# Attention and feed-forward in one kernel: a written order of 712 pieces up to the second chunk, own buffers for the first four pairs, maxima subtracted by TensorE

## The chip, the cores and the metric

The kernel runs on one core of a Trainium2 chip. The metric is the device time of one execution in microseconds (us). Three executions of the kernel before gave 937.13, 939.01 and 940.65 us; their median, 939.01 us, is the time before. The engines are called by their names in the profile: PE (TensorE, with its weight loads PEld), DVE (VectorE), ACT (ScalarE), POOL (GpSimd) and SP (SyncE, which issues the transfers).

## The reference

For 8 batches, 8 heads, 576 positions and head dimension 64, two attentions are added: one over pooled positions (means of 4, so 144 of them, repeated 4 times in the output) and one over a band of |i-j| < 4. Their sum, 4608 rows of 512, goes through a feed-forward layer with 2048 hidden units and a piecewise quadratic gate.

```python
out_d = sm_attn(q_d, k_d, v_d)              # pooled by 4
out_up = np.repeat(out_d, factor, axis=2)
scores = scale * np.matmul(q, k.transpose(0, 1, 3, 2))
scores = np.where(np.abs(pos[:, None] - pos[None, :]) < factor, scores, -1000000000.0)
...                                         # softmax, then @ v
x = (out_up + out_local).transpose(0, 2, 1, 3).reshape(4608, 512)
h = x @ w_in
g = np.where(h >= 1, h, np.where(h <= -1, 0.0, (h + 1) ** 2 / 4.0))
return g @ w_out
```

## The kernel before

**Attention.** Heads go in pairs: 32 pairs, four for each batch. For a pair, the band scores are formed in ten windows of 64 (`sl_ps`, L224), the pooled scores in three blocks of 48 rows (`sp_ps`, L259). DVE takes the maxima (L243 or L249, L275, L276) and subtracts the band maxima (L244; for pairs 4 to 7 POOL does, L250), ACT takes the exponentials (L251, L279), DVE normalises (L288 to L294), PE turns the weights (`tl_ps` L313, `tp_ps` L325), ACT copies them (L317, L331), PE multiplies them with the values (`pl_ps`, L357 and L369), and DVE adds the two attentions to `x` (L380). ACT rounds `x` to `xh` (L396) and POOL forms the rest `xl = x - xh` (L397), so that a float32 product can be made of three products of rounded parts. The sums of four queries and keys are `qd` (L199) and `kd` (L203); those of the values are `vd` (POOL, L306 and L307; DVE, L301, for pairs 4 to 7).

**Feed-forward.** Weights come as 32 blocks of 512 KB (`raw_i`, `raw_o`, loaded by L592) and are converted: ACT scales both words (L604, L606), DVE shifts and adds (L609, L610), ACT rounds (L612), POOL forms the rest (L613). The tokens go in chunks: chunk 0 has 512, then come eight of 384 and two of 512. For a chunk and one of 16 blocks of hidden units, `mm1` makes 12 products into `h_ps` (L679), the gate runs on DVE, ACT, DVE, ACT and POOL (for chunk 0 L694, L695, L696, L705, L706; later chunks have a copy L699 ahead), and `mm2` makes 12 (or 9) products into `o_ps` (L722). Later chunks overlap with the attention of pairs 8 to 31, which `join` runs one step behind another at the steps listed in `JOINS`.

**What sets the order.** Before chunk 1 the program is traced in the order of two lists of short steps (`BEFORE_STEPS` for pairs 0 to 3, `FIRST_STEPS` for pairs 4 to 7 beside chunk 0; `a0` is the next stage of pair 0, `w` a load of two weight blocks, `c` a conversion, `s` one `mm1` with its gate, `m` one `mm2`), and a scheduler then sorts the instructions of each engine by its own estimates. Every engine takes its instructions strictly in the order of its own queue; an instruction that waits holds all behind it on that engine, and on SP a load that waits for a buffer holds all later loads. Pairs 1 and 3 borrow buffers of late weight blocks (`second`), pairs 0 and 2 share another set; all four share one buffer for `v` and one for the pooled `v`. PSUM has four double banks for pairs 0 to 3; afterwards two banks hold `h_ps`, four `o_ps`, and one double bank the attention.

Of the kernel before, what the change touches and what calls it, by code (L numbers as in the profile page):

```python
# [62 lines left out]
def place(h, g):  # L63
# [39 lines left out]
JOINS = [17, 20, 23, 26, 30, 37, 44, 51, 58, 65, 69, 73, 78, 84, 91, 98, 105, 113, 117, 121, 125]  # L103
JOINS += [129, 133, 137, 142]
# [14 lines left out]
def attention_then_ffn(ctx: ExitStack, tc, qT, kT, vw, vp, vq, band, w_in, w_out, out):  # L119
# [25 lines left out]
    def load(n, name):  # L145
# [16 lines left out]
        loaded[name] = t
# [25 lines left out]
    def attention(n, pool):  # L188

        b, p = pairs[n]  # L190
        q, k = qk[p] if b == 0 else (loaded["q"], loaded["k"])
        copy = nc.scalar.copy


        qd = first_qd
        if n < NPAIR and n % 2:
            qd = scratch(n, [P, NQB * QB + D - QB], "qd", "qd")
            nc.gpsimd.memset(qd[:, SD:], 0.0)
# [4 lines left out]
        nc.vector.tensor_reduce(kd, k.rearrange("p (s f) -> p s f", f=FACTOR), axis=AX.X, op=ALU.add)  # L203
# [16 lines left out]
        for h, r, g in SCORE_ORDER:  # L220
            w = WIN_START[r * NG + g]
            hs = slice(h * D, (h + 1) * D)
            x, c = place(h, g), (2 * g + r) * WIN
            nc.tensor.matmul(  # L224
                sl_v[x * WIN : (x + 1) * WIN, c : c + WIN],
                q[hs, w : w + WIN],
                k[hs, w : w + WIN],
                start=not early,
                stop=True,
                skip_group_check=early,  # L230
            )
        if n + 1 >= NPAIR:
            load(n + 1, "q")
            load(n + 1, "k")
        yield

        sl = scratch(n, [P, NG, 2, WIN], "sl", "sl")
        slf = sl.rearrange("p g r c -> p (g r) c")
        sl_n = sl_v.rearrange("p (n c) -> p n c", c=WIN)
        ml = small(NB, "mxl")  # L240
        ml_n = ml.unsqueeze(2).broadcast_to([P, NB, WIN])
        if early:
            nc.vector.tensor_reduce(ml, sl_n, axis=AX.X, op=ALU.max)  # L243
            nc.vector.tensor_tensor(slf, sl_n, ml_n, op=ALU.subtract)  # L244
        else:
            nc.vector.tensor_tensor(
                slf, sl_n, band_sb.unsqueeze(1).broadcast_to([P, NB, WIN]), op=ALU.add
            )
            nc.vector.tensor_reduce(ml, slf, axis=AX.X, op=ALU.max)  # L249
            nc.gpsimd.tensor_tensor(slf, slf, ml_n, op=ALU.subtract)  # L250
        nc.scalar.activation(slf, slf, AF.Exp, scale=0.125)  # L251
        yield
        sp_ps = pool.tile([P, 2, 512], F32, name="sp_ps", tag="a")
        sp_v = sp_ps[:, 0, 0 : 2 * SD].rearrange("p (n s) -> p n s", n=2)
        sp_w = sp_ps[:, 1, 0:SD]
        for i in (0, 2, 1):
            for h in range(2):
                hs = slice(h * D, (h + 1) * D)
                nc.tensor.matmul(  # L259
                    sp_v[hs, i, :] if i < 2 else sp_w[(1 - h) * D : (2 - h) * D, :],  # L260
                    qd[hs, i * QB : i * QB + D],
                    kd[hs, :],
                    start=True,
                    stop=True,
                )
# [9 lines left out]
        nc.vector.tensor_reduce(mx_ps[:, 2:3], sp_w, axis=AX.X, op=ALU.max)  # L275
        nc.vector.tensor_reduce(mx_ps[:, 0:2], sp_v, axis=AX.X, op=ALU.max)  # L276
# [12 lines left out]
        nc.vector.tensor_scalar_add(sums, sums, 1e-9)
        nc.vector.reciprocal(sums, sums)  # L290
        nc.vector.tensor_tensor(
            slf, slf, sums[:, 0:NB].unsqueeze(2).broadcast_to([P, NB, WIN]), op=ALU.mult
        )
        nc.vector.tensor_tensor(  # L294
# [540 lines left out]
```

## Time and profile before

| what | value |
|---|---|
| median of three runs | 939.01 us |
| the profiled execution, device time | 938.05 us |
| its span, first to last instruction | 936.3 us |
| mean granted PE clock over the span | 0.976 |
| PE, DVE, ACT, POOL busy | 894.3, 494.6, 460.2, 380.1 us |
| bytes moved by the DMA engines | 68.59 MB |

The device time is 1.75 us above the span. In the rows of the profile an arrow points from inputs to the output (`o_ps<-w_o,gh`), the times of one instruction are nanoseconds, and the figures behind a bar are busy time and mean. Window rows give, for each stretch, the busy time of every engine with its instructions in brackets, then the granted PE clock, the share of the DMA engines and GB/s.

### The profile page before, as it was taken

To read this page: it belongs to the slowest core of one execution; us is meant where nothing else is said; L and a number is where in the kernel's file an instruction comes from. 1 tells how busy PE (TensorE), PEld (TensorE's weight loads), DVE (VectorE), ACT (ScalarE), POOL (GpSimd) and SP (SyncE) were. 2 spreads that over 40 slices of the span, in tenths; PEclk is the share of its full clock that TensorE was granted. 3 is DMA by queue.
4 is the path that set the end of the run, shared out by engine and by line. 5 is a ranking of instruction groups with operands and counts; after the bars stand their busy time and mean duration, and the time that the engine had idled before them with its cause. 6 is when DMAs were issued, how large, how long until landed. Compare 5 with 4: busy or idle time off the path is not lost.

```text
span 936.3 us, 18293 instructions
## 1 busy us (share of the span) xinstructions
PE 894.3 (96%) x7420; PEld 795.4 (85%) x7420; DVE 494.6 (53%) x884; ACT 460.2 (49%) x987; POOL 380.1 (41%) x346
## 2 busy tenths in 40 slices
PE   4689899999999999999999999999999999999997
PEld 4567677888999999989999999998998988888886
DVE  5978788567543554366544553456676521212221
ACT  4889554445544444445444444454454443334333
POOL 2647576445433444344433443344544422222221
PEclk7669999999999999999999999999999999999999
DMA  8786111232120121032120121022231000001001
GB/s 293 258 311 210 51 31 39 92 93 79 57 91 1 57 91 57 3 129 75 57 75 18 57 91 40 18 91 75 81 106 57 15 35 1 1 1 46 1 1 45
DMA packets 27973, 68.59 MB, mean 73 GB/s; under 512 B 3248, under 2 KB 3248, under 8 KB 27888
## 3 DMA queue, kind: packets, MB, share of 16 engines
q1 hardware_dynamic: 27888, 67.42, 21.8%
q8 instruction: 58, 0.95, 0.4%
q14 instruction: 27, 0.22, 0.1%
HBM read 57.97 MB, written 9.44 MB: 72 GB/s over the span
## 4 chain that ended last, share of the span: by engine, by line
PE 76%; DVE 8%; issue 5%; DMA 4%; POOL 3%; ACT 3%; SPq 0%; POOLq 0%; ACTq 0%; DVEq 0%
PE h_ps L679 34%; PE o_ps L722 34%; PE join_ps L440 2%; DVE m L609 2%; DVE m L610 2%; PE turn_ps L570 2%; PE join_ps L455 1%; PE turn_ps L572 1%; POOL gl L706 1%; PE join_ps L466 1%; DMA raw_o<-w_out 1%; PE join_ps L428 1%; DMA out<-osb 1%; DMA first_i<-qT 1%; POOL xl L397 1%
## 5 line engine op out<-in xcount | busy, mean ns | idle before, releaser
L706 POOL TENSOR_TENSOR gl<-u,gh 128x384 fp32r<-128x384 f32 (+1 forms) x176 | 193.5, 1099 | 442.6 <-ACT gh L705 365.6
L679 PE MATMUL h_ps<-xh,w_i 128*128 128x384 f32 (+1 forms) x1408 | 368.0, 343 | 0.0
L722 PE MATMUL o_ps<-w_o,gh 128*128 128x512 f32 x1152 | 348.1, 383 | 2.4 <-ACT gh L705 2.4
L679 PEld LDWEIGHTS h_ps<-xh,w_i 128*128 128x128 f32 x1408 | 254.9, 190 | 16.4 <-issue 0.4
L679 PE MATMUL h_ps<-xl,w_i 128*128 128x384 f32 (+1 forms) x704 | 240.8, 342 | 0.5 <-POOL xl L397 0.5
L722 PEld LDWEIGHTS o_ps<-w_o,gh 128*128 128x128 f32 x1152 | 212.8, 189 | 33.3 <-issue 5.8
L722 PE MATMUL o_ps<-w_o,gl 128*128 128x512 f32 x576 | 219.6, 381 | 4.0 <-POOL gl L706 4.0
L700 DVE TENSOR_SCALAR u<-m 128x384 f32<-128x384 f32 (+1 forms) x160 | 60.3, 377 | 292.3 <-ACT m L699 281.2
L705 ACT CAST gh<-u 128x384 fp32r<-128x384 f32 (+1 forms) x176 | 95.5, 543 | 128.9 <-DVE u L702 124.4
L702 DVE SCALAR_TENSOR_TENSOR u<-m,u 128x384 f32<-128x384 f32 (+1 forms) x160 | 113.2, 707 | 83.9 <-ACT u L701 83.9
L699 ACT COPY m<-h_ps 128x384 f32<-128x384 f32 (+1 forms) x160 | 80.1, 501 | 124.5 <-PE h_ps L679 121.4
L679 PEld LDWEIGHTS h_ps<-xl,w_i 128*128 128x128 f32 x704 | 133.3, 189 | 6.5 <-POOL xl L397 1.1
L701 ACT ACTIVATE u<-u 128x384 f32<-128x384 f32 (+1 forms) x160 | 87.2, 545 | 102.1 <-DVE u L700 102.1
L722 PEld LDWEIGHTS o_ps<-w_o,gl 128*128 128x128 f32 x576 | 109.2, 190 | 21.2 <-POOL gl L706 5.6
L397 POOL TENSOR_TENSOR xl<-x,xh 128x576 fp32r<-128x576 f32 (+6 forms) x44 | 56.9, 1303 | 45.4 <-ACT xh L396 45.2
L532 ACT ACTIVATE sl<-sl 128x640 f32<-128x640 f32 x24 | 17.7, 738 | 55.3 <-POOL sl L506 55.3
L506 POOL TENSOR_TENSOR sl<-sl,mxl 128x640 f32<-128x640 f32 x24 | 30.2, 1260 | 5.1 <-DVE mxl L505 5.1
L613 POOL TENSOR_TENSOR w_i<-m,w_i 128x512 fp32r<-128x512 f32 x16 | 23.3, 1457 | 21.3 <-ACT w_i L612 21.3
L613 POOL TENSOR_TENSOR w_o<-m,w_o 128x512 fp32r<-128x512 f32 x16 | 25.0, 1565 | 17.0 <-ACT w_o L612 17.0
L534 ACT ACTIVATE sp<-join_ps,mxp 128x144 f32<-128x144 f32 x72 | 26.9, 380 | 0.0
L396 ACT CAST xh<-x 128x576 fp32r<-128x576 f32 (+6 forms) x44 | 22.9, 545 | 4.8 <-DVE x L380 4.3
L559 POOL TENSOR_TENSOR vh<-vq_sb 128x384 f32<-128x384 f32 x24 | 24.8, 1035 | 0.0
(109 smaller groups left out, 855.9 us busy)
## 6 DMA issues: line engine op xcount, KB each, us to landing
v_sb<-vw SPq DMA_DIRECT2D x32, 320.0 KB, 3.0
vq_sb<-vq SPq DMA_DIRECT2D x24, 384.0 KB, 3.1
out<-osb SPq DMA_DIRECT2D x36, 256.0 KB, 2.4
raw_i<-w_in SPq DMA_DIRECT2D x16, 512.0 KB, 6.8
raw_o<-w_out SPq DMA_DIRECT2D x16, 512.0 KB, 7.4
q_sb<-qT SPq DMA_DIRECT2D x28, 288.0 KB, 3.3
k_sb<-kT SPq DMA_DIRECT2D x28, 288.0 KB, 4.1
vp_sb<-vp SPq DMA_DIRECT2D x8, 288.0 KB
```

The costliest lines, as they stand in the source:

```text
L397: nc.gpsimd.tensor_tensor(xl[:, p, dst], x[:, part], xh[:, p, dst], op=ALU.subtract)
L506: shifted = nc.gpsimd.tensor_tensor(slf, slf, ml.unsqueeze(2).broadcast_to([P, NB, WIN]), op=ALU.subtract)
L534: nc.scalar.activation(sp[:, i], sp_v[i], AF.Exp, bias=mx[:, j : j + 1], scale=scale, accum_out=sums[:, NB + i : NB + i + 1],)
L613: nc.gpsimd.tensor_tensor(w[:, 1], m, w[:, 0], op=ALU.subtract)
L679: ins = nc.tensor.matmul(h, wi[:, wt, cc * P : (cc + 1) * P], turns(xt[:, cc, ts]), start=(n == 0), stop=(n == 3 * NCC - 1),)
L699: nc.scalar.copy(m, h)
L700: nc.vector.tensor_scalar(u, m, -1.0, 1.0, op0=ALU.max, op1=ALU.add)
L701: nc.scalar.activation(u, u, AF.Square, scale=0.5)
L702: nc.vector.scalar_tensor_tensor(u, m, 1.0, u, op0=ALU.max, op1=ALU.min)
L705: nc.scalar.copy(gh, u)
L706: nc.gpsimd.tensor_tensor(gl, u, gh, op=ALU.subtract)
L722: ins = nc.tensor.matmul(o, gt[:, ts], turns(wo[:, wt, :]), start=f == 0 and n == 0, stop=f == NFC - 1 and n == 2)
```

## The change

**A written order.** The two lists of steps give way to one string, `ORDER`, of 712 pieces: single loads, single instructions or one short group of products. `0.sl@hi1` is the band scores of pair 0 in the PSUM double bank `hi1`, `i0.c3` the third piece of the conversion of weight block i0, `f3.s2` the products of hidden block 3 with pair 2's rows, `f3.u1` the first piece of its gate, `m3.2` the third quarter of its second product. The scheduler is switched off for this part, so each engine's queue is the string's order. It runs up to the last product of chunk 0 and the first `mm1` of chunk 1 (`f16`). Two lines of it, and the manual loop in short:

```diff
+ORDER = """
+    0.lq 0.z 0.lk 1.lq 1.z 1.lk 0.qd 0.lp 0.sl@hi1 0.kd 0.lv 1.qd 0.sp@hi0 0.mx 2.lq 2.z
...
+    m13.2 f15.gh m14.1 f15.gl m13.3 m14.2 m15.0 m14.3 m15.1 f16.s1 m15.2 f16.s2 m15.3 f16.s3
+""".split()
...
+    with tc.tile_pool(name="up", bufs=1, space=bass.MemoryType.PSUM) as up, tc.manual_schedule():
...
+        for token in ORDER:
```

**Buffers.** Pairs 1, 2 and 3 each get five buffers of their own out of the weight blocks 4 to 11, for `v` and the pooled `v` too; the loads of 15 of those weight blocks therefore stand behind these pairs. Block o11 is free. The buffers of `m`, `u`, `osb` (4), `gh` (3) and `gl` (3) become one ring of ten.

```diff
+    slots = iter([f"w{x}{f}" for f in range(4, 12) for x in "io"])
+    place_of = {
+        "sl": (0, 0), "vd": (0, 640), "x": (0, 0), "al": (1, 0), "xd": (1, 640),
+        "sp": (2, 0), "vh": (2, 432), "ap": (2, 432), "v": (3, 0), "vp": (4, 0),
+    }
...
+        return mpool.tile([P, 512], F32, name=name, tag="t512", bufs=10)
```

**Work moved between engines.** For pairs 0 to 3, TensorE subtracts the band maxima: DVE takes them negated, and a float32 product with the identity adds them to the scores in PSUM. For pairs 4 to 7 the band is added by TensorE, as it was for pairs 0 to 3, and DVE subtracts instead of POOL. The sums of queries and keys of pairs 1 to 3 go from DVE to POOL, as two additions each. One maximum over all pooled blocks takes the place of two. The pooled values of pairs 4 to 7 are laid out by the host so that the four addends are neighbours.

```diff
+            if 0 < n < NPAIR:
+                half = loaded[name, n][:, 736:1024].rearrange("p (s f) -> p s f", f=2)
+                nc.gpsimd.tensor_tensor(half, src[:, :, 0:2], src[:, :, 2:4], op=ALU.add)
+                nc.gpsimd.tensor_tensor(dst, half[:, :, 0], half[:, :, 1], op=ALU.add)
+            else:
+                nc.vector.tensor_reduce(dst, src, axis=AX.X, op=ALU.add)
...
+                t["ml"], t["sl_v"].rearrange("p (n c) -> p n c", c=WIN), axis=AX.X, op=ALU.max, negate=early
...
+                    nc.tensor.matmul(
+                        v[:, c0 - SL0 : c1 - SL0],
+                        ident,
+                        t["ml"][:, (c0 - SL0) // WIN : (c1 - SL0) // WIN]
+                        .unsqueeze(2).broadcast_to([P, (c1 - c0) // WIN, WIN]),
+                        start=False,
...
+            nc.vector.tensor_reduce(t["mx_ps"], t["sp_all"], axis=AX.X, op=ALU.max)
...
+    inner = pooled[1].reshape(NPAIR, KB, NKB, FACTOR, 2 * D).transpose(0, 1, 2, 4, 3)
```

**Groups.** In the second part only the steps of `JOINS` change; the products keep their order.

```diff
-JOINS = [17, 20, 23, 26, 30, 37, 44, 51, 58, 65, 69, 73, 78, 84, 91, 98, 105, 113, 117, 121, 125]
-JOINS += [129, 133, 137, 142]
+JOINS = [17, 20, 23, 26, 30, 37, 44, 51, 58, 63, 68, 73, 78, 85, 92, 99, 106, 111, 115, 120, 125]
+JOINS += [130, 134, 138, 142]
```

**What moves: DVE in the opening.** This is a stretch of DVE's queue before, ahead of the first `mm1`. `raw_o_211` and `raw_i_253` are weight blocks, `sl_396` is pair 3's band scores, `x` the first result.

```order
L609 TENSOR_SCALAR m<-raw_o_211 128x512
L275 TENSOR_REDUCE sp_ps<-sp_ps 128x1
L610 ISA m<-raw_o_211,m 128x1024
L276 TENSOR_REDUCE sp_ps<-sp_ps 128x2
L380 TENSOR_TENSOR x<-pl_ps,xd 128x576
L277 TENSOR_SCALAR mxp<-sp_ps 128x3
L243 TENSOR_REDUCE mxl<-sl_ps 128x10
L609 TENSOR_SCALAR m<-raw_i_253 128x512
L244 TENSOR_TENSOR sl_396<-sl_ps,mxl 128x640
L610 ISA m<-raw_i_253,m 128x1024
```

And this is the same place, from pair 3's band maxima on, in the changed kernel; `own_...` are the pairs' own buffers, `raw_i_279` is weight block i0, the first to be converted.

```order
L316 TENSOR_REDUCE mxl<-sl_ps 128x10
L391 RECIPROCAL sp_ps<-sp_ps 128x13
L395 TENSOR_TENSOR own_2_282<-own_2_282,sp_ps 128x640
L400 TENSOR_TENSOR own_2_293<-own_2_293,sp_ps 128x432
L740 TENSOR_SCALAR m<-raw_i_279 128x512
L366 TENSOR_REDUCE sp_ps<-sp_ps 128x3
L370 TENSOR_SCALAR mxp<-sp_ps 128x3
L743 ISA m<-raw_i_279,m 128x1024
L385 TENSOR_REDUCE sp_ps<-own_3_401 128x10
```

The subtraction behind the maxima (L244) is gone from DVE, and only one weight block's shift and addition stand here; those of seven others have gone behind the four pairs.

**What moves: SP.** Before, weight blocks alternate with the pairs' shared buffers; `raw_i_516` and `raw_o_518` are blocks i3 and o3, `raw_i_737` is i4.

```order
L592 DMA raw_i_516<-w_in 128x1024
L592 DMA raw_o_518<-w_out 128x1024
L161 DMA v_sb<-vw 128x640
L155 DMA vp_sb<-vp 72x1024
L592 DMA raw_i_737<-w_in 128x1024
L592 DMA raw_o_739<-w_out 128x1024
```

Now, from block i3 on; `raw_o_655` is o11, `raw_i_672` is i9, and `raw_i_682` is i4.

```order
L723 DMA raw_i_563<-w_in 128x1024
L723 DMA raw_o_603<-w_out 128x1024
L194 DMA q_sb<-qT 128x576
L194 DMA k_sb<-kT 128x576
L197 DMA vp<-vp 72x1024
L723 DMA raw_o_655<-w_out 128x1024
L723 DMA raw_i_672<-w_in 128x1024
L723 DMA raw_i_682<-w_in 128x1024
L723 DMA raw_o_694<-w_out 128x1024
```

The load of i9 goes into a buffer that pair 3 uses to its end (`xl` on POOL is its last reader), that of i4 into one of pair 1's. The 21 other weight blocks, o4 first, stand behind these two.

**What moves: PE at the end of chunk 0.** Before, the first `mm1` of chunk 1 (`w_i_227`, 384 columns) is followed by the last second products of chunk 0 (`w_o_1808`), and then by the next `mm1` (`w_i_415`).

```order
L679 MATMUL h_ps<-xh,w_i_227 128x384 x2
L679 MATMUL h_ps<-xl,w_i_227 128x384
L722 MATMUL o_ps_813<-w_o_1808,gh 128x512 x2
L722 MATMUL o_ps_813<-w_o_1808,gl 128x512
L722 MATMUL o_ps_810<-w_o_1808,gh 128x512 x2
L722 MATMUL o_ps_810<-w_o_1808,gl 128x512
L722 MATMUL o_ps_811<-w_o_1808,gh 128x512 x2
L722 MATMUL o_ps_811<-w_o_1808,gl 128x512
L722 MATMUL o_ps_812<-w_o_1808,gh 128x512 x2
L722 MATMUL o_ps_812<-w_o_1808,gl 128x512
L679 MATMUL h_ps<-xh,w_i_415 128x384 x2
```

Now these stand so; `ffn_lo_605` holds in its first bank the `h` of both `w_i_473` and `w_i_601`, which are blocks i0 and i1.

```order
L770 MATMUL ffn_lo_605<-xh,w_i_473 128x384 x2
L770 MATMUL ffn_lo_605<-xl,w_i_473 128x384
L824 MATMUL ffn_hi_626<-w_o_1608,gh 128x512 x2
L824 MATMUL ffn_hi_626<-w_o_1608,gl 128x512
L770 MATMUL ffn_lo_605<-xh,w_i_473 128x384 x2
L770 MATMUL ffn_lo_605<-xl,w_i_473 128x384
L770 MATMUL ffn_lo_605<-xh,w_i_601 128x384 x2
```

The last products of chunk 0 have moved in between the pieces of the first `mm1`, so that two `mm1` into the same bank now follow one another.

More of the change, by code (lines that the diff above doesn't have):

```diff
@@ L248, in attention @@
             )
[L249 to L264, printed above, removed]
-                )
@@ L364, in attention @@
-        load(n + 1, "v")
-        pp_v = pl_ps[:, 0, 0:SD]
-        for kb in range(NKB):
-            for h in range(2):
-                hs = slice(h * D, (h + 1) * D)
-                put(nc.tensor.matmul(
-                    pp_v[hs, :],
-                    vd[:, kb, hs],
-                    ap[:, kb, :, h, :],
-                    start=(kb == 0),
-                    stop=(kb == NKB - 1),
-                ))
-        yield
-        xd = scratch(n, [P, SD], "xd", "kd")
-        nc.scalar.mul(xd, pp_v, 1.0 / FACTOR)
@@ new lines, in pp, with xd @@
+        def pp():
+            vd = t["vd"].rearrange("k (n c) -> k n c", n=NKB)
+            for kb in range(NKB):
+                for h in range(2):
+                    hs = slice(h * D, (h + 1) * D)
+                    nc.tensor.matmul(
+                        t["pl_ps"][hs, 0, 0:SD],
+                        vd[:, kb, hs],
+                        t["ap"][:, kb, :, h, :],
+                        start=(kb == 0),
+                        stop=(kb == NKB - 1),
+                    )
+        def xd():
+            t["xd"] = scratch(n, "xd", [P, SD])
+            nc.scalar.mul(t["xd"], t["pl_ps"][:, 0, 0:SD], 1.0 / FACTOR)
@@ new lines, in gates, with mm1, second_product @@
+    def gates(c, f):
+        with tc.high_priority(offset=100):
+            for piece in ("u1", "sq", "u2", "gh", "gl"):
+                gate(c, f, piece)
+    def mm1(c, f):
+        for cc in range(NCC):
+            product(c, f, cc)
+        gates(c, f)
+    def second_product(c, f, t):
+        gh, gl = gtiles[c, f]
+        o = places["o"](t)
+        ts = slice(t * P, (t + 1) * P)
+        for n, (gt, wt) in enumerate(((gh, 0), (gh, 1), (gl, 0))):
+            ins = nc.tensor.matmul(
+                o, gt[:, ts], turns(weights["o", f][:, wt, :]),
+                start=f == 0 and n == 0, stop=f == NFC - 1 and n == 2,
+            )
+            if c > 0 and n == 0:
+                tc.keep_in_program_order(ins)
+        if f == NFC - 1:
+            osb = temp("osb")
+            nc.scalar.copy(osb, o)
+            rows = out[CHUNKS[c][0] : CHUNKS[c][0] + CHUNKS[c][1], :].rearrange("(a b) d -> b a d", a=2)
+            nc.sync.dma_start(rows[t * P // 2 : (t + 1) * P // 2], osb)
@@ L745, in attention_then_ffn @@
+    steps = [(c, f) for c in range(1, len(CHUNKS)) for f in range(NFC)]
+    first, second = iter(steps[1:]), iter(steps)
+    gates(*steps[0])
     with tc.tile_pool(name="ps_g", bufs=1, space=bass.MemoryType.PSUM) as ps_g:
-        places["h"] = ps_h
+        places["h"] = lambda f: bank(low, "lo0", 0)
         pooled_sums(SECOND)
@@ L749, in attention_then_ffn @@
         for n in range(NFC + 1, (NMID + 1) * NFC + 1):
-            mm1(*next(todo["s"]))
+            mm1(*next(first))
             if n in JOINS:
```

667 lines of the change are left out of this document (377 added, 290 removed).

## The prediction

> **What bounds the kernel now.** The page's busy shares come first, then its 40 slices, to see where PE is not busy.
>
> ```profile
> PE 894.3 (96%) x7420; PEld 795.4 (85%) x7420; DVE 494.6 (53%) x884; ACT 460.2 (49%) x987; POOL 380.1 (41%) x346
> ...
> PE   4689899999999999999999999999999999999997
> ...
> DVE  5978788567543554366544553456676521212221
> ...
> PEclk7669999999999999999999999999999999999999
> ```
>
> PE is the bound from the third slice on. The first two (23 us each) have PE half idle at a clock of 0.6 to 0.7, while DVE is fullest. The timeline of PE gives the ends of the stages: the first product of chunk 0, and the last.
>
> ```profile
> 55.67 1.55 PE L224 MATMUL sl_ps<-k_sb,q_sb 64*64 64x64 f32 x40 [1.33 <-DVE x L380]
> 57.15 1.22 PE L679 MATMUL h_ps<-xh,w_i 128*128 128x512 f32 x2
> ...
> 173.30 0.38 PE L722 MATMUL o_ps<-w_o,gl 128*128 128x512 f32 x1
> 173.52 0.49 PE L679 MATMUL h_ps<-xh,w_i 128*128 128x384 f32 x2
> ```
>
> Cut there, the windows show three stages.
>
> ```profile
> core 0: us, PE busy (x) PEld busy (x) DVE busy (x) ACT busy (x) POOL busy (x), PEclk, DMA share, GB/s
> 0.00:57.15 57.15, 33.39 (x512) 26.86 (x512) 42.09 (x71) 40.24 (x93) 26.94 (x33) 0.68 0.82 274
> 57.15:173.50 116.35, 108.74 (x802) 88.06 (x801) 91.92 (x137) 72.74 (x136) 69.84 (x50) 0.97 0.31 106
> 173.50:936.30 762.80, 752.18 (x6109) 680.48 (x6107) 360.59 (x676) 347.23 (x760) 283.37 (x264) 1.00 0.16 53
> ```
>
> Call them opening (57.15 us), chunk 0 (116.35) and rest (762.80). In the opening DVE works 42.09 us and waits 15.06. In the rest PE is all but full, and the change leaves its products alone. So the gain has to come from the first 173.5 us.
>
> **The opening.** These DVE rows lie in it.
>
> ```profile
> L610 DVE CUSTOM_DVE_ANT_0 m<-raw_o,m 128x1024 uint16<-128x1024 uint16 x4 | 4.8, 1208 | 0.0
> L610 DVE CUSTOM_DVE_ANT_0 m<-raw_i,m 128x1024 uint16<-128x1024 uint16 x4 | 3.4, 853 | 0.0
> L609 DVE TENSOR_SCALAR m<-raw_i 128x512 int32<-128x512 int32 x4 | 3.3, 830 | 4.1 <-ACT raw_i L604 4.1
> L244 DVE TENSOR_TENSOR sl<-sl_ps,mxl 128x640 f32<-128x640 f32 x4 | 3.3, 814 | 0.0
> L203 DVE TENSOR_REDUCE kd<-first_o 128x144 f32<-128x576 f32 x4 | 2.9, 737 | 0.0
> L609 DVE TENSOR_SCALAR m<-raw_o 128x512 int32<-128x512 int32 x4 | 2.6, 658 | 0.0
> L294 DVE TENSOR_TENSOR sp<-sp,sp_ps 128x432 f32<-128x432 f32 x4 | 2.4, 594 | 0.0
> L301 DVE TENSOR_REDUCE vd<-vp_sb 72x256 f32<-72x1024 f32 x1 | 2.0, 1983 | 0.0
> L276 DVE TENSOR_REDUCE sp_ps<-sp_ps 128x2 f32<-128x288 f32 x4 | 1.8, 456 | 0.0
> L275 DVE TENSOR_REDUCE sp_ps<-sp_ps 128x1 f32<-128x144 f32 x4 | 1.2, 289 | 0.0
> ```
>
> Ahead of chunk 0 the new order keeps 3 of the 16 conversion pieces (14.1 us in four rows): 11.5 us go. Six sums of queries and keys go to POOL (6 x 0.74 = 4.4), the four subtractions to PE (3.3), pair 4's `vd` behind the four pairs (2.0). One maximum over 432 columns, at 0.59 as the 432-column row L294, replaces 0.46 and 0.29: 0.6 in four. Together 21.8 us in 30 instructions; neighbours overlap in these rows (the durations exceed the busy window), so I take 20.5. DVE then works 21.6 us. With its old waits of 15.1 the opening lasts 36.7 us.
>
> PE is nearer to being the limit. What it does in the opening stays, and the subtraction by product is new, 640 columns for each of four pairs.
>
> ```profile
> L313 PE MATMUL tl_ps<-ident,sl 128*128 128x128 f32 x20 | 4.7, 390 | 12.4 <-DVE sl L291 12.4
> L655 PE MATMUL warm<-ident 128*128 128x128 f32 x20 | 4.6, 429 | 1.7 <-POOL qd L198 1.7
> ```
>
> Four times 640 columns of transposes cost 4.7 us, ten float32 products of 128 columns (20 records) 4.6, or 2.3 for 640. So 1.2 to 2.3 a pair; 1.75, the middle, since both are for `ident` at a mixed clock, makes 7 us. PE would need 33.4 + 7.0 = 40.4 us at the old mean clock of 0.68, and 27.5 at full clock; it starts at 1.7. POOL's twelve additions are bounded by a 256-column and a 512-column addition in the rows below: 0.73 and 1.39 for two halves of a sum, so at most 2.8 us a sum and some 1.2 by columns, 7 us in all; they have cover, for POOL is busy 26.9 of 57 us now and loses seven conversions at 1.4 (L613).
>
> ```profile
> L613 POOL TENSOR_TENSOR w_i<-m,w_i 128x512 fp32r<-128x512 f32 x4 | 5.7, 1430 | 6.1 <-ACT w_i L612 6.1
> L306 POOL TENSOR_TENSOR vh<-vp_sb 72x512 f32<-72x512 f32 x4 | 5.6, 1388 | 13.8 <-DMA vp_sb<-vp 9.5 <-PE pl_ps L357 4.3
> L307 POOL TENSOR_TENSOR vd<-vh 72x256 f32<-72x256 f32 x4 | 2.9, 726 | 0.2
> ```
>
> I take 40 us for the opening, 3.3 above DVE's figure for waits on a half-cold PE; bounds 36.7 and 47 (half of DVE's saving coming back as such waits). Gain: 17.1 us.
>
> **Chunk 0.** What left the opening comes here. DVE: 91.9 + 11.5 for conversions, + 1.3 for pair 4's `vd`, which with addends as neighbours should cost nearer the 0.74 of a 576-element sum than 1.98 (estimate 1.3; bounds 0.74 and 1.98), - 2.1 for the three others, - 0.6 for merged maxima: 102.0. Behind DVE's last gate piece stand a rounding, a POOL rest and the last twelve products.
>
> ```profile
> L705 ACT CAST gh<-u 128x512 fp32r<-128x512 f32 x16 | 9.9, 619 | 4.0 <-DVE u L696 3.9
> ...
> L706 POOL TENSOR_TENSOR gl<-u,gh 128x512 fp32r<-128x512 f32 x16 | 22.0, 1377 | 12.7 <-ACT gh L705 8.7 <-issue 3.2 <-POOL xl L397 0.8
> ...
> L250 POOL TENSOR_TENSOR sl<-sl,mxl 128x640 f32<-128x640 f32 x4 | 5.2, 1305 | 1.1 <-DVE mxl L249 1.1
> ```
> ```profile
> 760.13 2.59 PE h_ps L679 x12
> ```
>
> That is 4.6 us; so DVE's floor is 106.6. PE's: 32 dozens at 2.59, 82.9, one of 384 columns, under 2.6, and the attention, whose share of PE's window is what the lines L679 (first row) and L722 (second) leave of 108.74: 10.8.
>
> ```profile
> 57.15:173.50 116.35, 49.38 (x204) 39.09 (x205) 0.97 0.31 106
> ...
> 57.15:173.50 116.35, 48.53 (x192) 35.65 (x192) 0.97 0.31 106
> ```
>
> With some 1.5 for the bands of pairs 5 to 7, PE needs about 98 us. So DVE is the limit, which before was idle 24.4 us here; ACT, 72.7 us busy, has room for the conversions that it gets. The conversion pieces depend on POOL: this is DVE, then POOL.
>
> ```profile
> 41.05 0.41 DVE L609 TENSOR_SCALAR m<-raw_i 128x512 int32<-128x512 int32 x1
> ...
> 42.92 1.51 DVE L609 TENSOR_SCALAR m<-raw_i 128x512 int32<-128x512 int32 x1
> ```
> ```profile
> 42.34 2.27 POOL L397 TENSOR_TENSOR xl<-x,xh 128x512 fp32r<-128x512 f32 x2 [1.85 <-ACT xh L396]
> ```
>
> The same shift takes 0.41 us with POOL idle and 1.51 beside a POOL subtraction. POOL's busy share rises from 60% (69.8 of 116) to about 70% (78 of 112: seven conversions in at 1.4, four L250 out, 5.2, and some `xl` in). A piece averages 0.89 in the opening's four rows against 0.55 quiet (0.41 here; 0.68 at best for L610, an estimate from its 0.85), so a sixth more excess, 0.06 on 61 pieces: 3.5 us. [...]
>
> One new wait is on DVE's path: i4's load stands on SP behind i9's, which needs pair 3's last `xl`; DVE's shift of i4 holds later gates. POOL gets there some 7 us into chunk 0 (five rests at 1.4), DVE after twenty pieces at some 0.7, 14 us; the transfer and ACT's two pieces lie between. A stall of 0 to 4 us, I take 1.5. Both with DVE's floor make 111.6; bounds 106.6 and 118 (half of the old waits kept on top). I take 112, a gain of 4.4.
>
> **The rest.** Two `mm1` in one bank meet at the border: behind the last product stand the copy of `o` (0.59) and that of `h` (0.48), less 0.5 of PE's work; I take 0.9 us lost (0 to 1.5).
>
> ```profile
> L699 ACT COPY m<-h_ps x160: 467/479/588, 171.1 to 924.7; 128x384 f32<-128x384 f32 x128, 128x512 f32<-128x512 f32 x32
> ```
> ```profile
> L729 ACT COPY osb<-o_ps x36: 567/585/606, 171.8 to 931.8; 128x512 f32<-128x512 f32 x36
> ```
>
> The moved groups touch PE's waits for attention, of which this is the largest in the rest; zero, with 3 us either way. The ring of ten replaces ten buffers: zero; a block's gate is covered by two dozens of products, 5.2 us, and 0.1 us uncovered at each of the 160 later blocks would cost 16.
>
> ```profile
> PE turn_ps L570 <- DVE sp L186: 2.4, 3, 1.0
> ```
>
> **Sum.** 17.1 + 4.4 - 0.9 = 20.6 us off the profiled execution's 938.05 (0.96 under the median): 917.4.
>
> **The rivals.** *Opening stays cold* (0.10): PE, not DVE, sets the opening. At a clock of 0.5 its 40.4 us become 55, from 1.7 on 56.6, so only chunk 0 gains: 938.05 - 0.6 - 4.4 + 0.9 = 934. For it: the clock of 0.68. Against it: PE waited 12.4 us there for one DVE line, which has less ahead of it now. [...]
>
> *POOL holds DVE* (0.13): all 61 pieces cost 1.21, the dearest kind's mean above: 61 x 0.32 = 20 us more than 106.6, chunk 0 takes 126.6. Then 938.05 - 17.1 + 10.3 + 0.9 = 932. [...] Against it: 40% of POOL's time was free.
>
> *Convoy* (0.08, slower): the strict order makes PE wait for a gate at each of 16 blocks, since `gh` and `gl` now stand behind conversions on ACT and POOL, where the scheduler put gates first. PE's 98 us leave 18 us of loss now, 1.1 per block. From 2.2 per block on the change is slower; at 3, chunk 0 lasts 146 and the time is 938.05 - 17.1 + 29.7 + 0.9 = 951.6. Against it: two `h` banks and ten buffers let two blocks be in flight.
>
> *Nothing much* (0.07): shorter waits in the opening return as waits for DMA, which at 274 GB/s already carries 15.7 MB in 57 us; a 40 us opening gets 11 MB, and chunk 0 waits for weights: 938.
>
> **Chances.** Forecast 0.62. The range, 906 to 935, takes the forecast's bounds (36.7 and 106.6 give 908, less 2 for the groups; 47 and 118 give 930) and the two mild rivals. A measurement of this kernel can tell 0.5%, 4.7 us. Faster by more: forecast, POOL rival and most of the cold one, 0.83; within it, 0.09; slower, 0.08.
>
> **What would show it.** First product of chunk 0 at about 40 us and end of chunk 0 at about 152; DVE over 85% busy between; no POOL L250-like subtraction there. Wrong if the opening's PE clock stays under 0.7, if the mean of a conversion piece exceeds 1.1 us, or if PE waits over 2 us a block for `gh` or `gl`.

## The result, and the profile after

The changed kernel takes 1046.76 us (median of 4 runs, 1044.63 to 1048.52) beside 938.46 us for the kernel before (4 runs). The ratio is 1.115, with a 95% interval of 1.112 to 1.1181. It is 108 us slower, where 917.4 was forecast. The profiled execution took 1048.52 us with a span of 1046.7.

The busy shares and slices of the changed kernel's page come first.

```profile
PE 930.7 (89%) x7444; PEld 791.4 (76%) x7444; DVE 476.1 (45%) x866; ACT 466.6 (45%) x987; POOL 379.0 (36%) x356
...
PE   8689999998998999899898899799989989998997
PEclk9899999999999999999999999999999999999999
```

Two things differ from before. The cold stretch at the start is mostly gone: the clock's first tenths were 7 and 6 and are 9 and 8 now. But the row of nines that PE had to the end is broken by eights and sevens all along. The stages show it in us. They are cut as before: at the first product of chunk 0, and at the first product of chunk 1's second `mm1`, which starts at 159.92.

```profile
core 0: us, PE busy (x) PEld busy (x) DVE busy (x) ACT busy (x) POOL busy (x), PEclk, DMA share, GB/s
0.00:36.83 36.83, 30.70 (x531) 24.32 (x531) 23.65 (x45) 21.13 (x55) 20.47 (x36) 0.95 0.89 281
36.83:159.92 123.09, 108.15 (x810) 88.66 (x807) 91.52 (x145) 95.12 (x174) 75.51 (x57) 0.97 0.42 149
159.92:1046.70 886.78, 791.89 (x6108) 678.42 (x6108) 360.89 (x678) 350.32 (x759) 282.96 (x264) 0.99 0.14 45
```

The opening gained 20.3 us (57.15 to 36.83), chunk 0 lost 6.7 (116.35 to 123.09), and the rest lost 124.0 (762.80 to 886.78). The rest has the same products: 6108 records, 6109 before. PE's largest waits in it are these; a row gives who waited for whom, then the us in total, the number of waits and the longest.

```profile
PE ffn_lo L824 <- ACT m L789: 59.4, 103, 0.7
PE ffn_lo L824 <- ACT osb L832: 17.3, 10, 3.2
PE ffn_hi L824 <- ACT m L789: 11.6, 16, 0.7
```

A step is one `mm1` and one second product (`mm2`, L824). In 119 of 160 steps the first product of the second product waits for ACT's copy of `h` (`m`, L789). It doesn't read that copy. PE's timeline in one such step:

```profile
401.08 0.49 PE L770 MATMUL ffn_lo<-xh,w_i 128*128 128x384 f32 x2
401.41 0.33 PE L770 MATMUL ffn_lo<-xl,w_i 128*128 128x384 f32 x1
402.30 0.70 PE L824 MATMUL ffn_lo<-w_o,gh 128*128 128x512 f32 x2 [0.57 <-ACT m L789]
402.84 0.38 PE L824 MATMUL ffn_lo<-w_o,gl 128*128 128x512 f32 x1
...
404.35 0.49 PE L770 MATMUL ffn_lo<-xh,w_i 128*128 128x384 f32 x2
```

ACT's copy in the same step:

```profile
401.77 0.48 ACT L789 COPY m<-ffn_lo 128x384 f32<-128x384 f32 x1 [2.08 <-PE ffn_lo L770]
```

And a step of the kernel before, from the last product of its `mm1` on.

```profile
401.31 0.33 PE L679 MATMUL h_ps<-xl,w_i 128*128 128x384 f32 x1
401.47 0.59 PE L722 MATMUL o_ps<-w_o,gh 128*128 128x512 f32 x2
401.90 0.38 PE L722 MATMUL o_ps<-w_o,gl 128*128 128x512 f32 x1
```

Before, products follow each other at starts 0.16 us apart here (401.31, 401.47), and the copy of `h` runs beside 1.94 us of second products. Now PE stops until the copy ends: 402.30 instead of 401.57 (0.16 behind 401.41) is 0.73 us, and the first pair takes 0.54 to the next start instead of 0.43, 0.11 more. The waits' row counts 0.57 of it. The rest, lost overlap, is booked as busy time: PE's busy time in this stage rose by 39.7 us for the same products, and its idle time by 84.3; together 124.0.

Why there? In the changed kernel `h` and `o0` are the two banks of one tile, `ffn_lo0`. The compiled program puts the wait for ACT (`Activation`) here, in one step of the changed kernel:

```
L770 MATMUL ffn_lo_605<-xl,w_i_1000 128x384
L824 MATMUL ffn_lo_605<-w_o_885,gh 128x512 [waits Activation_49]
```

and there, in the same step of a variant where they are two tiles (`own_banks`, below):

```
L824 MATMUL o_1970<-w_o_885,gh 128x512 x2
...
L770 MATMUL h_1867<-xh,w_i_984 128x384 [waits Activation_49]
```

### The profile page after: what moved, and what is told of

Read it like the earlier page. It is cut to its first block, busy times and chain, and to the rows that moved or that the text cites. A ratio compares the mean times of both kernels' runs of the same rounds, so it can differ in the third digit from the quotient of the medians.

```text
span 1046.7 us, 18187 instructions
## 1 busy us (share of the span) xinstructions
PE 930.7 (89%) x7444; PEld 791.4 (76%) x7444; DVE 476.1 (45%) x866; ACT 466.6 (45%) x987; POOL 379.0 (36%) x356
## 3 DMA queue, kind: packets, MB, share of 16 engines
q1 hardware_dynamic: 27888, 67.42, 19.4%
## 4 chain that ended last, share of the span: by engine, by line
PE 61%; ACT 13%; issue 10%; DVE 10%; POOL 5%; DMA 0%; POOLq 0%; ACTq 0%; SPq 0%; DVEq 0%
PE ffn_lo L824 26%; PE ffn_lo L770 20%; ACT m L789 6%; PE ffn_hi L770 5%; DVE u L796 4%; POOL sl L638 3%; ACT sp L666 2%; PE ffn_hi L824 2%; POOL gl L806 2%; PE turn_ps L702 1%; ACT sl L664 1%; ACT osb L832 1%; PE turn_ps L704 1%; DVE sl L682 1%; ACT gh L803 1%
## 5 line engine op out<-in xcount | busy, mean ns | idle before, releaser
L824 PE MATMUL ffn_lo<-w_o,gh 128*128 128x512 f32 x1056 | 332.1, 396 | 80.3 <-ACT m L789 59.4
L770 PE MATMUL ffn_lo<-xh,w_i 128*128 128x384 f32 (+1 forms) x1216 | 310.9, 338 | 0.8 <-ACT m L789 0.6
L824 PEld LDWEIGHTS ffn_lo<-w_o,gh 128*128 128x128 f32 x1056 | 187.3, 189 | 146.4 <-ACT m L789 97.1
L770 PEld LDWEIGHTS ffn_lo<-xh,w_i 128*128 128x128 f32 x1216 | 217.8, 190 | 12.7 <-ACT m L789 0.9
L770 PE MATMUL ffn_lo<-xl,w_i 128*128 128x384 f32 (+1 forms) x608 | 203.7, 335 | 0.0
L824 PE MATMUL ffn_lo<-w_o,gl 128*128 128x512 f32 x528 | 200.8, 380 | 0.0
L789 ACT COPY m<-ffn_lo 128x384 f32<-128x384 f32 (+1 forms) x144 | 70.4, 489 | 179.9 <-PE ffn_lo L770 179.9
L770 PEld LDWEIGHTS ffn_lo<-xl,w_i 128*128 128x128 f32 x608 | 115.2, 190 | 2.5
L824 PEld LDWEIGHTS ffn_lo<-w_o,gl 128*128 128x128 f32 x528 | 100.3, 190 | 14.2
L770 PE MATMUL ffn_hi<-xh,w_i 128*128 128x512 f32 x192 | 59.1, 391 | 0.6 <-DVE u L796 0.6
L824 PE MATMUL ffn_hi<-w_o,gh 128*128 128x512 f32 x96 | 30.3, 397 | 11.6 <-ACT m L789 11.6
L824 PEld LDWEIGHTS ffn_hi<-w_o,gh 128*128 128x128 f32 x96 | 16.7, 189 | 19.7 <-ACT m L789 18.0
```

What stands on the lines that cost most here:

```text
L770: ins = nc.tensor.matmul(htiles[c, f], wi[:, wt, cc * P : (cc + 1) * P], turns(xt[:, cc, ts]), start=(cc == 0 and xt is xh and wt == 0), s ...
L789: nc.scalar.copy(m, h)
L824: ins = nc.tensor.matmul(o, gt[:, ts], turns(weights["o", f][:, wt, :]), start=f == 0 and n == 0, stop=f == NFC - 1 and n == 2,)
```

## The experiments

**Theory and rivals.** The theory, "one tile, one wait": what writes one half of a double-bank tile is ordered behind what reads the other half, though they are different banks. Rivals: ACT's reading of one bank slows PE in the next one; the ring of ten makes gates late; the moved groups cost. Four kernels tell them apart. Each ratio below is to the kernel before, timed again beside the variant; its medians there are 937.81 to 939.07 us.

`own_banks` gives `h`, `o0`, `o1`, `o2` single-bank tiles after chunk 0.

```diff
     gates(*steps[0])
+    early.close()
+    rest = ctx.enter_context(tc.tile_pool(name="rest", bufs=1, space=bass.MemoryType.PSUM))
...
-        places["h"] = lambda f: bank(low, "lo0", 0)
+        places["h"] = lambda f: single(rest, "h0")
+        places["o"] = lambda t: single(rest, f"o{t}")
```

> The changed kernel, but from the second mm1 of chunk 1 on h, o0, o1 and o2 (and the second h and o3 of the last part) are single-bank tiles of their own instead of halves of double banks; same banks, same order of the products, same groups. Theory (one tile, one wait: the first product into o0 waits for ACT's copy m of h because both are halves of one tile): the rows ffn_lo L824 <- ACT m L789 (59.4 us) and <- ACT osb L832 (17.3 us) vanish, the part from the first product of the second mm1 (159.9 us) to the end goes from 886.8 back to before's 762.8 us, so 159.9 + 762.8 + 1.8 = 924.5, range 920 to 929. Rival neighbouring banks (ACT reading one bank slows PE writing the next): no recovery, about 1045. Rival ring of ten (gates late for want of a buffer) and rival moved groups: both unchanged by this edit, so about 1045.

Measured: 923.48 us, ratio to before 0.9843 (0.9817 to 0.9868). Its three stages:

```profile
0.00:36.42 36.42, 30.21 (x530) 23.65 (x531) 24.19 (x45) 21.02 (x55) 20.81 (x36) 0.95 0.89 284
36.42:157.82 121.40, 108.03 (x810) 88.04 (x806) 90.62 (x145) 95.64 (x174) 77.26 (x57) 0.97 0.43 151
157.82:920.50 762.68, 752.78 (x6108) 680.50 (x6108) 360.78 (x678) 344.12 (x759) 283.57 (x264) 1.00 0.16 52
```

The rest is back at before's 762.80 within 0.12 us. Ring, groups and order of the products stayed, so none of them cost the 124 us. The rival of the neighbouring banks falls too: as built, `h` and `o0` lie in banks 2 and 3 of the changed kernel and in banks 0 and 1 of `own_banks`. The banks are not the same ones, as the expectation says, but they are neighbours in both. (`six_banks`, below, has them in 2 and 3 again, and its rest takes 762.95 us.) The changed kernel did have `h` and the first `o` of a step in different banks, and in 119 of 160 steps PE waited for the copy all the same; here the tiles had to be different too.

`own_banks_old_groups` also takes back the list of groups.

```diff
-JOINS = [17, 20, 23, 26, 30, 37, 44, 51, 58, 63, 68, 73, 78, 85, 92, 99, 106, 111, 115, 120, 125]
-JOINS += [130, 134, 138, 142]
+JOINS = [17, 20, 23, 26, 30, 37, 44, 51, 58, 65, 69, 73, 78, 84, 91, 98, 105, 113, 117, 121, 125]
+JOINS += [129, 133, 137, 142]
```

> own_banks with the kernel before's list JOINS, nothing else. The prediction priced the moved groups at 0, 3 us either way. Theory (one tile, one wait): as own_banks within 3 us. Rival moved groups (they are what costs): own_banks stays near 1045 and this one falls to about 924.

Measured: 922.10 us, 0.983 (0.9799 to 0.9862). The moved groups are worth nothing that this measurement can tell, as priced.

`before_shared` puts the suspected cause into the kernel before: from the second `mm1` of chunk 1 on, `h` and `o0` are the two halves of one tile, in banks 0 and 1, where the kernel before has them as two tiles.

```diff
+    early.close()
+    shared["ps_o"] = ctx.enter_context(tc.tile_pool(name="rest", bufs=1, space=bass.MemoryType.PSUM))
+    shared["pair"] = shared["ps_o"].tile([P, 2, 512], F32, name="pair", tag="pair")
...
-        places["h"] = ps_h
+        places["h"] = Half()
```

> The kernel before, with one edit from its second mm1 of chunk 1 on: h and o0 are the two halves of one double-bank tile. Its scheduler, rings of 4, 3 and 3 buffers and old groups stay. Theory (one tile, one wait): the loss appears here too, 886.8 - 762.8 = 124 us in the changed kernel, some less where a group stands between: 938 + 115 = 1053, range 1035 to 1065. Rivals ring of ten and moved groups: nothing happens, 938.

Measured: 1031.46 us, 1.0983 (1.0967 to 1.0999); 92 us lost, 4 us under the expected range. Its rest and the wait in it:

```profile
173.50:1030.10 856.60, 783.69 (x6115) 677.81 (x6114) 360.99 (x677) 354.67 (x763) 283.20 (x264) 1.00 0.14 47
```
```profile
PE pair L729 <- ACT m L704: 63.4, 103, 0.9
```

The same 103 waits appear, with before's scheduler, rings and groups. The theory holds in both directions. The expectation took over 115 of the 124 us, although this kernel joins neither `o1` with `o2` nor the last part's second `h` with `o3`.

`o0_last` keeps the tiles and changes the order of the quarters.

```diff
-        for t in (3, 0, 1, 2) if CHUNKS[c][1] == 512 else (0, 1, 2):
+        if CHUNKS[c][1] == 512:
+            order = (3, 1, 2, 0) if f % 2 else (0, 1, 2, 3)
+        else:
+            order = (1, 2, 0)
+        for t in order:
```

> The changed kernel, tiles as they are, but each second product from chunk 1 on takes its quarters in another order: the quarter that shares a tile with the newest h comes last (o1, o2, o0; in the last part o0, o1, o2, o3 or o3, o1, o2, o0). Theory (one tile, one wait): the copy of h has 1.3 us of other products (two quarters at 0.65) to run beside, instead of none, and takes some 0.9 with its start; the waits on m vanish; what is left is the wait on the copies osb at 8 chunk ends, some 1 us each: 924.5 + 8 = 932, range 924 to 938. Rival neighbouring banks: PE still writes beside the copy, but another pair of banks; a part recovers, 980 to 1030. Rivals ring of ten and moved groups: about 1045.

Measured: 972.76 us, 1.0373 (1.032 to 1.0427). The direction is right and the size a miss by 41 us. The waits on `m` all but vanished; what is left is not 8 us but this.

```profile
PE ffn_lo L824 <- ACT osb L832: 27.0, 10, 5.0
```

PE's timeline at a chunk's end:

```profile
395.71 0.38 PE L824 MATMUL ffn_lo<-w_o,gl 128*128 128x512 f32 x1
400.35 1.22 PE L824 MATMUL ffn_lo<-w_o,gh 128*128 128x512 f32 x2 [4.26 <-ACT osb L832]
401.36 0.63 PE L824 MATMUL ffn_lo<-w_o,gl 128*128 128x512 f32 x1
```

ACT there:

```profile
399.30 0.51 ACT L803 CAST gh<-u 128x384 fp32r<-128x384 f32 x1 [0.62 <-DVE u L796]
399.72 0.58 ACT L832 COPY osb<-ffn_lo 128x512 f32<-128x512 f32 x1
```

The product into `o2` waits for the copy of `o1`, the other half of its tile. That copy stands in ACT's queue behind the newest block's whole gate (`m`, square, `gh`, each waiting for DVE), so it starts 3.6 us after the last product into `o1` has ended. And after the wait the products take 1.22 and 0.63 us where those ahead of it took 0.59 and 0.38 (from 395.28 on).

**Taking the 124 us apart.** `o12_pair` and `h1o3_pair` each put one pair back into `own_banks`.

```diff
+        if name in ("o1", "o2"):
+            return bank(pool, "o12", name == "o2")
```

> own_banks with only o1 and o2 put back as the two halves of one tile, after chunk 0. It takes the loss of 124 us apart: before_shared, which joins only h0 and o0, lost 92. Theory (one tile, one wait): at a chunk's end the first product into o2 waits for ACT's copy of o1, which stands in ACT's queue behind the newest block's gate. In the changed kernel this was the row ffn_lo L824 <- ACT osb L832, 17.3 us in 10 waits; with some 0.3 us of lost overlap each the run takes 923.5 + 20 = 943, range 935 to 950. Rival (the waits of osb only followed from the waits on m): 923.5.

Measured: 963.39 us, 1.0261 (1.0245 to 1.0277): 40 us lost, twice what was expected. One row has 25.5 us of it. The other row is the stage behind chunk 0, to be read beside the third one of `own_banks`.

```profile
PE ffn_o L824 <- ACT osb L832: 25.5, 10, 4.9
158.44:961.50 803.06, 768.68 (x6108) 692.40 (x6108) 360.89 (x678) 345.66 (x759) 283.19 (x264) 0.98 0.15 50
```

The stage is 40.4 us longer. PE's idle time there rose by 24.5 us, and its busy time by 15.9 (752.78 to 768.68) with as many records, at a granted clock of 0.98 instead of 1.00. So the part that the expectation lacked is products at a lower clock behind the waits, as in `o0_last`; there PE's busy time in this stage is 767.66 us, 14.9 above `own_banks`, and the mean granted clock of the run 0.985 against 0.994.

```diff
+        if name in ("h1", "o3"):
+            return bank(pool, "h1o3", name == "h1")
```

> own_banks with only the last part's second h and o3 put back as the two halves of one tile. Theory (one tile, one wait): the row ffn_hi L824 <- ACT m L789 of the changed kernel comes back, 11.6 us in 16 waits, and 0.3 us of lost overlap each: 923.5 + 16 = 939.5, range 933 to 945. With 92 from before_shared and 20 from o12_pair that makes 128, against the 124 lost. Rival (only the first bank pair is at fault): 923.5.

Measured: 940.49 us, 1.0028 (1.0009 to 1.0047): 17 us lost, as expected. Each pair costs by itself, but 92 + 40 + 17 = 149 is more than 124: the parts don't add. The ten waits for `osb` are 17.3 us in the changed kernel and 25.5 in `o12_pair`, and the mean clock is 0.991 there against 0.977 here. A likely reason is that PE has already stood still for `m` before it comes to `o1` and `o2`, so that their copy is less late; no run tests it apart.

**Chunk 0.** With the rest settled, the forecast still misses 6 us: 923.5 against 917.4. `pe_less` and `dve_more` ask which engine limits chunk 0, from `own_banks`. The first leaves out the products with `xl` in chunk 0, so it computes less.

```diff
+            if c == 0 and xt is xl:
+                continue
```

> own_banks without the products with xl in chunk 0: each of its 16 mm1 leaves out four of twelve products, so the first output rows lose accuracy, and 16 x 4 x 0.216 = 13.8 us of PE's work go while DVE, ACT and POOL keep theirs. It asks what limits chunk 0, which took 121.4 us in own_banks (36.4 to 157.8) against the predicted 112. PE limits it (its rows there need some 107 us, not the 98 of the prediction): the stage falls by 10 to 14 us, to about 109, and the time to 912. DVE limits it, as the prediction said: the stage stays within 3 us of 121, the time near 922.

```diff
             nc.vector.tensor_scalar(mi, t[:, :, 1], 3, None, op0=ALU.logical_shift_left)
+            if f > 1:
+                nc.vector.tensor_scalar(mi, t[:, :, 1], 3, None, op0=ALU.logical_shift_left)
```

> own_banks with DVE's shift (piece 3) done twice for the 28 weight blocks i2 to i15 and o2 to o15, the second writing the same values: 28 x 0.42 to 0.60 = 12 to 17 us more work on DVE in chunk 0, nothing elsewhere. PE limits chunk 0: DVE waits 31 of 121 us there, most of the extra is absorbed, the stage grows by 0 to 6 us, time 922 to 929. DVE limits it, as the prediction said: it grows by 12 to 17 us, time 935 to 940.

Measured, one run each: 919.36 and 941.95 us, the second just above the range for a limit by DVE. Chunk 0 in `pe_less`:

```profile
36.11:154.84 118.73, 98.87 (x746) 78.47 (x743) 92.25 (x145) 92.64 (x174) 76.27 (x57) 0.94 0.44 155
```

Chunk 0 in `dve_more`, and the added rows:

```profile
36.41:177.23 140.82, 115.83 (x810) 92.73 (x806) 110.62 (x173) 95.02 (x174) 74.73 (x57) 0.92 0.37 130
```
```profile
L742 DVE TENSOR_SCALAR m<-raw_o 128x512 int32<-128x512 int32 x14 | 10.9, 776 | 0.5
...
L742 DVE TENSOR_SCALAR m<-raw_i 128x512 int32<-128x512 int32 x14 | 7.6, 546 | 0.5
```

Products worth 13.8 us less on PE (its busy time fell by 9.2) shorten the stage by 2.7; 18.5 us more on DVE lengthen it by 19.4. Six executions with the same chunk 0 took 121.15 to 123.09 us, so the first is little more than their spread and the second is far beyond it. Added DVE work goes on in full, although DVE is idle 31 us of the stage: that idle time is not free. The reading is that it lies in a chain through the engines.

`six_banks` uses single-bank tiles from chunk 0 on.

```diff
+            if token == "f0.s0":
+                ops[3]["x"]()
+                early.close()
+                pools["rest"] = ctx.enter_context(psum("rest", reuse_waits="tile"))
+                pools["mid"] = middle.enter_context(psum("mid", reuse_waits="tile"))
```

> own_banks, with h0, h1, o0, o1, o2 and o3 as single-bank tiles from the first product of chunk 0 on, so that no two of them share a tile anywhere. Same order on every engine. In chunk 0 of own_banks three rows name a wait between the two halves of one tile: PE's L824 for DVE's u (2.2 us), and DVE's u for PE's L824 (1.8 and 0.6). If the sharing costs there too, they go and the stage falls by 2 to 5 us, time 919 to 921; if PE's own work limits the stage and those waits lie beside it, nothing: 923.

Measured: 921.54 us, 0.9813 (0.9796 to 0.9829). That is not clear of `own_banks` (922.21 to 927.46) or `own_banks_old_groups` (920.25 to 927.56). Its chunk 0 takes 119.98 us, 1.4 less than in `own_banks`. The sharing costs little there.

`scheduled` takes the strict order away.

```diff
-    with tc.tile_pool(name="up", bufs=1, space=bass.MemoryType.PSUM) as up, tc.manual_schedule():
+    with tc.tile_pool(name="up", bufs=1, space=bass.MemoryType.PSUM) as up:
```

> own_banks with the scheduler left on for the first part: the same pieces, tiles and buffers, but each engine's queue is the scheduler's order again, not the string's. It asks why chunk 0 took 121.4 us instead of 112. If the strict order makes engines wait for one another (the prediction's rival Convoy, in small), the stage from the first product of chunk 0 to the second mm1 of chunk 1 falls below 121 towards the predicted 112, and the time to 914 to 921. If the order is worth what it costs, the stage or the opening grows, and the time is 925 to 940. The rest stays at 763 in both.

Measured: 944.97 us, 1.0077 (1.005 to 1.0103), 5 us over the expected range and slower than the kernel before. Its first two stages:

```profile
0.00:47.95 47.95, 33.59 (x530) 26.54 (x530) 24.70 (x46) 28.52 (x71) 24.07 (x41) 0.89 0.83 256
47.95:181.06 133.11, 113.03 (x811) 89.34 (x807) 96.01 (x143) 83.22 (x158) 70.15 (x52) 0.95 0.34 123
```

Both grow, by 11.5 and 11.7 us. The written order doesn't cost chunk 0; without it this program would be no gain at all.

`opening_dve` undoes two parts of the change, on `own_banks`.

```diff
-            if 0 < n < NPAIR:
+            if False:
                 half = loaded[name, n][:, 736:1024].rearrange("p (s f) -> p s f", f=2)
...
             v = t["sl_v"]
-            if early:
+            if False:
```

> own_banks with two parts of the change undone: for pairs 0 to 3 DVE subtracts the band maxima again (4 x 0.81 = 3.3 us) instead of TensorE (5.9 us in own_banks), and DVE makes the sums of queries and keys of pairs 1 to 3 again (6 x 0.74 = 4.4 us) instead of POOL (6.6 us). The prediction's reading, that DVE's work sets the opening: the first product of chunk 0 moves from 36.4 to 42 to 44 us, the time to 929. Rival, that loads and the chain between engines set it: it stays within 2 us of 36.4 and the time near 922.

Measured, one run: 927.66 us. Its opening:

```profile
0.00:39.17 39.17, 28.33 (x515) 23.34 (x515) 30.28 (x55) 21.22 (x55) 14.12 (x24) 0.83 0.85 265
```

DVE has 6.1 us more work than in `own_banks`, and the opening is 2.75 us longer; chunk 0 is 123.4. The prediction's reading, 42 to 44 us, fails. The rival can't be decided: the opening with both parts in place took 36.11 to 39.04 us in eight executions, and this one run lies just above that. So 6.1 us of DVE's work are worth some 3 us of the opening at most (39.17 - 36.11), and perhaps nothing.

`six_banks_pe_sub` lets TensorE subtract for pairs 4 to 7 as well. In its order the exponential of these pairs stands ahead of their pooled scores (not shown).

```diff
-                t["ml"], t["sl_v"].rearrange("p (n c) -> p n c", c=WIN), axis=AX.X, op=ALU.max, negate=early
+                t["ml"], t["sl_v"].rearrange("p (n c) -> p n c", c=WIN), axis=AX.X, op=ALU.max, negate=True
...
-            if early:
+            if True:
```

> six_banks, with the subtraction of the band maxima on TensorE for pairs 4 to 7 too: 4 x 0.83 = 3.3 us leave DVE in chunk 0, some 4 x 1.5 = 5.9 us come to PE, and the exponential of these pairs stands ahead of the pooled scores, since both use the same double bank. If DVE's queue sets chunk 0 one for one (dve_more: 18.5 us more on DVE, 19.4 more in the stage) and PE's work counts a fifth (pe_less: 13.8 us less, 2.7 less), the stage falls by 3.3 - 1.2 = 2 us: 919.5, range 917 to 922. If PE has to wait for that exponential each time, nothing or a loss: 922 to 925.

Measured: 925.19 us, 0.9865 (0.9845 to 0.9886). Chunk 0 takes 124.3 us, 4.3 more than in `six_banks`, with 4.1 us less of DVE's work (86.64 against 90.71). So DVE's work alone does not set the stage. DVE's wait for the pooled scores grew, first in `six_banks`, then here.

```profile
DVE sp_ps L366 <- PE sp_ps L357: 0.4, 1, 0.4
DVE sp_ps L363 <- PE sp_ps L354: 3.8, 3, 2.4
```

This fits the exponential that now stands ahead of these scores. PE's busy time rose too, by 4.4 us (108.57 to 113.01), and no run separates the two.

## Why the prediction was wrong

**The step that failed** is the one on the rest: "the change leaves its products alone", with 0.9 us lost where "Two `mm1` in one bank meet at the border". The products were indeed the same. Their waits were not. The prediction looked at the shared tile at one place, where two `mm1` follow each other, and did not ask what else writes that tile: in each of the 128 steps of chunks 1 to 8 the second product begins with `o0`, in the tile that holds `h`, and in the last 32 steps with `o3`, in the tile that holds every second `h`. The term was -0.9 and measured -124.0. At the border itself, the one place that was priced, PE waited 0.6 us (0.9 was taken). `own_banks` and `before_shared` show the cause by taking it away and by adding it.

The prediction's own gauge was at hand: "0.1 us uncovered at each of the 160 later blocks would cost 16". What became uncovered was the copy `m`, 0.48 us, plus its start and lost overlap: 0.84 us, as in the step shown, at each of 119 steps is 100 us, an estimate; the waits on `osb` (17.3 us) make most of what remains.

**Opening.** Forecast 40, bounds 36.7 to 47; measured 36.83. PE's waits for the normalised weights fell from 12.4 us to 1.8, and the granted clock rose from 0.68 to 0.95; no run shows that the one brought the other. The clock of 0.5 in *Opening stays cold* is what the kernel before had from 40 to 60 us (0.50). The twelve POOL additions took 6.6 us against 7, the subtraction on PE 6.0 against 7. So the rivals *Opening stays cold* and *Nothing much* fail; for the second, no wait for a transfer stands in the rows of chunk 0. The sum behind 36.7 is less exact than its result. DVE worked 23.65 us, not 21.6: five conversion pieces and pair 4's `vd` fell in the opening, where three pieces and no `vd` were counted, and 26 instructions fewer are in it, not 30. Its waits were 13.2 us, not 15.1. The 12.4 us of PE's waits for one DVE line stood before three of the four groups of transposes (4.24, 3.94 and 4.21 us). `opening_dve` corrects the reading that DVE's work comes off one for one.

**Chunk 0.** Forecast 112, bounds 106.6 to 118; measured 123.09 here, 121.40 in `own_banks`. The failing step is "Both with DVE's floor make 111.6". The conversions, of both stages, are in these rows of before,

```profile
L610 DVE CUSTOM_DVE_ANT_0 m<-raw_o,m 128x1024 uint16<-128x1024 uint16 x16 | 17.9, 1122 | 0.1
L609 DVE TENSOR_SCALAR m<-raw_i 128x512 int32<-128x512 int32 x16 | 13.9, 871 | 4.1 <-ACT raw_i L604 4.1
L610 DVE CUSTOM_DVE_ANT_0 m<-raw_i,m 128x1024 uint16<-128x1024 uint16 x16 | 13.8, 862 | 0.0
...
L609 DVE TENSOR_SCALAR m<-raw_o 128x512 int32<-128x512 int32 x16 | 10.5, 654 | 0.0
```

and in these of the changed kernel.

```profile
L743 DVE CUSTOM_DVE_ANT_0 m<-raw_i,m 128x1024 uint16<-128x1024 uint16 x16 | 14.6, 944 | 0.0
L743 DVE CUSTOM_DVE_ANT_0 m<-raw_o,m 128x1024 uint16<-128x1024 uint16 x16 | 14.4, 929 | 0.0
L740 DVE TENSOR_SCALAR m<-raw_o 128x512 int32<-128x512 int32 x16 | 9.4, 602 | 0.4 <-ACT raw_o L734 0.4
L740 DVE TENSOR_SCALAR m<-raw_i 128x512 int32<-128x512 int32 x16 | 8.7, 566 | 0.6 <-ACT raw_i L734 0.6
```

A piece fell from 0.88 to 0.76 us (the mean of the four rows) instead of rising by 0.06, so *POOL holds DVE* fails, and DVE's work was 91.5 us, not 102, although that sum left out the four band subtractions of pairs 4 to 7 that the change gives to DVE (3.3 us). The stall for i4 was priced at 1.5; DVE's waits for ACT's pieces of the raw blocks are 1.0 us in all. Yet the stage was longer, because DVE's idle time was priced at 1.5 us plus a tail of 4.6 and was 31.6 (123.09 - 91.52). DVE was busy 74% of the stage, where over 85% was to show the forecast right. PE was busy 108.15 us, where 98 was worked out from dozens at 2.59; by `pe_less`, 13.8 us less of PE's work gave back only 2.7. An engine on a chain carries its waits with it: 24.4 us of idle time before was taken as room, and it came back. The largest waits of DVE in `own_banks` ahead of its last gate:

```profile
DVE u L790 <- PE ffn_hi L770: 4.4, 3, 2.8
DVE u L790 <- POOL gl L806: 4.0, 1, 4.0
DVE vd L419 <- PE pl_ps L476: 3.8, 3, 2.2
```

No single one carries it. The middle row is the ring of ten, for the last block's `u`. In `six_banks` the longest wait of the same instructions is 4.1 us for PE, and the stage is only 1.4 shorter, so the ring alone is not what costs. The largest row of PE's waits in the stage names DVE; the longest of the two waits ends at 49.29, at the transposes of pair 4's normalised weights.

```profile
PE tp_ps L438 <- DVE sl L395: 8.3, 2, 6.6
```

The kernel before has no such wait in chunk 0; its longest there is 1.6 us. What remains open is which of these waits could go; no order of the pieces that aims at them was tried.

**Convoy** was the rival on the slower side, with 951.6. It named waits of PE for `gh` or `gl` in chunk 0; none stands in PE's rows there. The run was slower for a wait in another stage, so that the side of this rival came true by luck, not by its mechanism, and `scheduled` shows the written order worth 21 us.

## What to carry to other kernels

Where buffers are merged into one tile, list for each half what writes it next, and what still reads the other half; the wait moves to the first writer of either (here 59.4 us in 103 waits of the first product into `o0`, for the copy of `h`). Read the waits beside the instructions of the compiled order, not only the instructions: an unchanged sequence of products can hold a new wait in most steps (119 of 160 here). An engine's busy time plus a little is no floor for a stage that is a chain through several engines: chunk 0 took 123.09 us where DVE, the limit in the forecast, was busy for 91.52.

## What the runs showed of the hardware

Long waits of PE can cost twice, once as idle time and once as products at half rate. In `o12_pair`, a wait of 2.40 us was followed by these products.

```profile
245.31 1.22 PE L824 MATMUL ffn_o<-w_o,gh 128*128 128x512 f32 x2 [2.40 <-ACT osb L832]
246.32 0.63 PE L824 MATMUL ffn_o<-w_o,gl 128*128 128x512 f32 x1
```

In the changed kernel, waits of 1.57 and of 3.18 us were followed by these.

```profile
253.38 0.70 PE L824 MATMUL ffn_lo<-w_o,gh 128*128 128x512 f32 x2 [1.57 <-ACT osb L832]
253.92 0.38 PE L824 MATMUL ffn_lo<-w_o,gl 128*128 128x512 f32 x1
...
680.24 0.70 PE L824 MATMUL ffn_lo<-w_o,gh 128*128 128x512 f32 x2 [3.18 <-ACT osb L832]
680.77 0.38 PE L824 MATMUL ffn_lo<-w_o,gl 128*128 128x512 f32 x1
```

After the first, the product took 0.63 us instead of 0.38; after the other two it kept 0.38, at a granted clock of 1.00 (253 to 255 and 680 to 682). In `o12_pair` the three other waits of 2.40 us led to half rate too, at once or some 1 us later, and one of 2.46 us did not; in the changed kernel waits of 2.40 and 2.47 us did as well, at a granted clock of 0.50 (424 to 426) and 0.52 (950 to 952). So the length of a wait alone doesn't decide in these rows: 2.40 us was enough five times, and 2.46 and 3.18 us were not. What else decides is not shown.
